# Sums of activations made over the second chunk and in the third chunk's first unit; the first down weights decoded two slots later

## The chip, the cores and the metric

The kernel runs on one core of a Trainium2 chip. The metric is the device time of one execution in microseconds (us). TensorE multiplies matrices (PE in the profile; PEld is its weight load), VectorE is DVE, ScalarE is ACT, GpSimd is POOL, and SP only issues transfers.

## The reference, cut to what matters

```
def phi(x):                                   # head_dim 64 -> 2 x 128 features
    proj = einsum('bhsd,df->bhsf', x, w_phi)
    proj = proj - max(abs(proj), axis=-1)
    return concatenate([exp(proj), exp(-proj)], axis=-1)
q_p, k_p = phi(q), phi(k)                     # batch 4, heads 8, seq 576
kv, z = einsum('bhsf,bhsd->bhfd', k_p, v), sum(k_p, axis=2)
attn = einsum('bhsf,bhfd->bhsd', q_p, kv) / (einsum('bhsf,bhf->bhs', q_p, z) + 1e-6)

x = attn as (2304 tokens, 512)
x = (sigmoid(x @ w_gate) * (x @ w_val)) @ w_out      # layer 1, d_ff 1536
h = x @ w_in2
out = maximum(0.01 * h, h) @ w_out2                  # layer 2, d_ff 2048
```

## The kernel before, in words

Every product of the two layers is made of three matmuls (`mm3`, L51 to L54): an operand is split into a high part that TensorE takes exactly and a low part that is the rest (`split`: a cast on ScalarE, L48, and a subtraction on VectorE, L49). The weights come from memory as 64-bit numbers and are decoded by `decode` (L97 to L114), per half of 128x512 six VectorE instructions (L102, L105, L107, L109, L111, L114) and two of ScalarE (L103, L112). `fetch` (L122) issues the load of such a half, `raw`.

Tokens stand as four blocks of 512 columns (b = 0 to 3, in two pairs) and a block B of 256 columns that holds the four rests. The hidden width is cut into chunks of 256: six chunks in layer 1, eight in layer 2. A chunk has the weights (layer, chunk, i) with i = 0 (gate), 1 (val), 2 (down).

The program has these parts, with the times of the profile before.

*Attention, 0 to about 290 us.* Sixteen pairs of heads run through slots; the order of the pieces in a slot is written by hand in `ORDERS` and `SLOTS` (L513 on). A piece `d` is one step of `first_weights`, which decodes chunk 0's three weights in slots 1 to 3; from slot KD = 4 on, pieces `M` run chunk 0's units of layer 1. `norm3` writes the attention's result to DRAM as `xd` as well.

*Chunk 0's rest and chunk 1, to about 395 us.* Plain units, one per block: `up_plain` (products into the banks `ps_u`, tanh on ScalarE L704, L706 on VectorE, `hidden`), then `down1_piece` per block and quarter (products into one of three banks `ps_p`). A down piece is copied by ScalarE into a staging half (L678) and added to DRAM by an accumulating transfer of POOL (L679, `accd`). There are six staging halves, used in turn.

*Chunks 2 to 5, to about 640 us.* For a pair of blocks `quad` makes the four products of 2x2 quarters out of seven instead of eight. It needs sums of weights (L176, L181) and sums of activations. The latter are made once for each pair: `load_x`-like transfers of SP bring `xd` into four tiles `acc` (L763, 512 KB each), `sum_steps` makes four subtractions on VectorE (L739), and `sum_parts` splits each result (ScalarE L749, VectorE L750); `store_sums` writes them to DRAM as `td`. Only one pair's sums are in SBUF at a time: `swap` loads the other pair's (L791, `w<-td`, on POOL) while a unit's products use up the old ones. Seven results are combined by additions of VectorE (L831). In chunk 1 all sums of layer 1 are made, pair 0's first, then pair 1's:

```
side.append(first_sums(0, False))
for b in range(NB):
    reserve[0] = (4, 8, 8, 5, 2)[b]
    if b == 2:
        for g in side:
            for _ in g:
                pass
        side[:] = [first_sums(1, True)]
    h = up_plain(1, 1, b, 5)
```

`side` holds generators whose steps `ahead` takes in between the units' pieces, beside one step of `stream`, which decodes the next weights as long as more than `reserve` of the 41 weight slots are free. A loop over `side` runs the rest of it at once.

*Step to layer 2, about 640 to 700 us.* In chunk 5 the sums of the down products stay in tiles `acc` (L682, added by VectorE), are split for block B and others (ScalarE L685, VectorE L686), and become the activations of layer 2, again with sums (L739, L749, L750): pair 0's four subtractions in the last unit, pair 1's four in front of layer 2.

*Layer 2, to the end.* Units of pair 0, block B and pair 1 per chunk, `quad` with one weight, results added by L901.

A tile framework's scheduler sets the static order on every engine; each engine then runs its instructions in that order.

## Time and profile before

| what | value |
| --- | --- |
| device time, three runs | 1053.50, 1058.68, 1058.72 us; median 1058.68 |
| the profiled execution | 1057.37 us |
| its span | 1055.6 us |
| mean granted TensorE clock | 0.997 |
| VectorE busy | 779.7 us |
| ScalarE busy | 519.4 us |

The span goes from the first to the last instruction that the profiler saw; the rest of the profiled execution's time lies around it. PEclk is the share of TensorE's full clock that was granted. In the table of stretches an engine's busy time stands beside the length of the stretch, so that the difference is its idle time there.

### The profile page before, as it was taken

The numbers are of one execution on the slowest core, as the hardware profiler recorded it, in microseconds if no ns is written. First come the engines' busy times: TensorE is split into PE (matmuls) and PEld (weight loads), VectorE is DVE, ScalarE is ACT, GpSimd is POOL, SyncE is SP. The second block draws the span as 40 slices with busy tenths as digits, with TensorE's granted clock in tenths as the row PEclk, the third lists the DMA queues.
The fourth block names the chain that finished last, engine by engine and source line by source line (L and its number), as shares of the span: only waits on it lengthen the run. The fifth ranks groups of instructions, "written<-read, shape, count | busy, mean of one in ns | idle before, by whom it ended". The sixth has DMA issues, their size and how long they took to land.

```text
span 1055.6 us, 15004 instructions
## 1 busy us (share of the span) xinstructions
PE 1024.2 (97%) x5410; PEld 870.9 (82%) x5410; DVE 779.7 (74%) x1373; ACT 519.4 (49%) x1066; POOL 170.2 (16%) x217
## 2 busy tenths in 40 slices
PE   8999999999999989999999999899999999999998
PEld 7788989889788778888888878688888888888886
DVE  4964878766489748396684959998797887979555
ACT  4766676767456535454454434477343333433221
POOL 0112121212201123324144120001010010101000
PEclk9999999999999999999999999999999999999999
DMA  6543344332287978759499494536161542515143
GB/s 146 157 98 90 88 101 108 82 104 75 74 296 226 343 141 246 114 145 262 73 239 195 82 317 182 182 139 228 52 237 71 171 149 91 178 62 179 42 165 133
DMA packets 119481, 160.06 MB, mean 152 GB/s; under 512 B 68720, under 2 KB 71408, under 8 KB 119408
## 3 DMA queue, kind: packets, MB, share of 16 engines
q1 hardware_dynamic: 95216, 94.09, 28.5%
q0 software_dynamic: 24192, 65.02, 24.6%
q8 instruction: 43, 0.70, 0.3%
q14 instruction: 30, 0.25, 0.1%
HBM read 109.64 MB, written 49.36 MB: 151 GB/s over the span
## 4 chain that ended last, share of the span: by engine, by line
PE 81%; DVE 8%; DMA 5%; ACT 3%; issue 2%; SPq 1%; POOL 1%; POOLq 0%; DVEq 0%; ACTq 0%
PE ps_u L53 11%; PE ps_u L52 11%; PE ps_u L54 11%; PE ps_p L52 11%; PE ps_p L54 11%; PE ps_p L53 11%; PE kv L395 4%; PE ps_n L445 2%; DMA raw<-in_moe_w_gate_dram 1%; DMA acc<-xd 1%; PE ps_t L328 1%; DVE w L750 1%; DVE ql L430 1%; DVE acc L739 1%; DMA w<-td 1%
## 5 line engine op out<-in xcount | busy, mean ns | idle before, releaser
L831 DVE TENSOR_TENSOR q<-ps_u,q 128x512 f32<-128x512 f32 x160 | 109.6, 686 | 65.6 <-PE ps_u L54 59.4
L53 PE MATMUL ps_u<-xl,w 128*128 128x512 f32 (+1 forms) x432 | 151.6, 351 | 0.3 <-DVE xl L686 0.3
L52 PE MATMUL ps_u<-xh,w 128*128 128x512 f32 (+1 forms) x432 | 151.4, 351 | 0.1
L54 PE MATMUL ps_u<-xh,w 128*128 128x512 f32 (+1 forms) x432 | 150.9, 350 | 0.0
L901 DVE TENSOR_TENSOR acc<-acc,ps_p 128x512 f32<-128x512 f32 x126 | 86.1, 684 | 39.6 <-PE ps_p L54 39.0
L52 PE MATMUL ps_p<-w,gh 128*128 128x512 f32 x288 | 112.2, 390 | 0.0
L53 PE MATMUL ps_p<-w,gh 128*128 128x512 f32 x288 | 112.0, 389 | 0.0
L54 PE MATMUL ps_p<-w,gl 128*128 128x512 f32 x288 | 111.7, 389 | 0.0
L791 POOL DMA_DIRECT2D w<-td x88 | 48.7, 560 | 380.6 <-PE ps_u L54 365.2
L679 POOL DMA_DIRECT2D accd<-w x80 | 70.8, 892 | 229.2 <-ACT w L678 148.3
L52 PE MATMUL ps_u<-w 128*128 128x512 f32 x256 | 100.2, 391 | 1.6 <-DVE q L831 1.6
L53 PE MATMUL ps_u<-w 128*128 128x512 f32 x256 | 99.9, 390 | 0.7 <-DMA w<-td 0.7
L54 PE MATMUL ps_u<-w 128*128 128x512 f32 x256 | 99.7, 389 | 0.0
L52 PEld LDWEIGHTS ps_u<-xh,w 128*128 128x128 f32 x432 | 81.9, 190 | 11.9 <-DVE q L831 0.5
L53 PEld LDWEIGHTS ps_u<-xl,w 128*128 128x128 f32 x432 | 82.0, 190 | 11.4 <-DVE xl L686 0.5
L54 PEld LDWEIGHTS ps_u<-xh,w 128*128 128x128 f32 x432 | 81.9, 190 | 10.9
L52 PE MATMUL ps_p<-gh,w 128*128 128x512 f32 (+1 forms) x216 | 79.3, 373 | 10.3 <-ACT gh L48 4.8
L467 POOL TENSOR_TENSOR rb<-u,rb 64x576 f32<-64x576 f32 x32 | 49.2, 1537 | 233.8 <-DMA rb<-rd 136.3
L717 ACT ACTIVATE q<-q 128x512 f32<-128x512 f32 x48 | 30.2, 632 | 111.9 <-DVE q L831 111.6
L53 PE MATMUL ps_p<-gl,w 128*128 128x512 f32 (+1 forms) x216 | 80.1, 372 | 0.4 <-DVE gl L49 0.4
L54 PE MATMUL ps_p<-gh,w 128*128 128x512 f32 (+1 forms) x216 | 79.7, 370 | 0.0
L49 DVE TENSOR_TENSOR gl<-q,gh 128x512 fp32r<-128x512 f32 (+1 forms) x102 | 61.8, 613 | 20.6 <-ACT gh L48 20.2
(151 smaller groups left out, 2306.0 us busy)
## 6 DMA issues: line engine op xcount, KB each, us to landing
w<-td POOLq DMA_DIRECT2D x88, 512.0 KB, 6.5
td<-w SPq DMA_DIRECT2D x32, 512.0 KB, 5.2
accd<-w POOLq DMA_DIRECT2D x64, 256.0 KB, 6.1
raw<-in_moe_w_out_dram SPq DMA_DIRECT2D x28, 512.0 KB, 4.8
raw<-in_moe_w_in_dram SPq DMA_DIRECT2D x16, 512.0 KB, 4.1
raw<-in_moe_w_gate_dram SPq DMA_DIRECT2D x12, 512.0 KB, 5.9
raw<-in_moe_w_val_dram SPq DMA_DIRECT2D x12, 512.0 KB, 5.1
rb<-rd SPq DMA_DIRECT2D x32, 144.0 KB, 3.2
```

Of the source, the lines that this page charges most:

```text
L49: nc.vector.tensor_tensor(out=lo, in0=src, in1=hi.bitcast(F32), op=ALU.subtract)
L52: nc.tensor.matmul(ps, lh, rh, start=first, stop=False, **kw)
L53: nc.tensor.matmul(ps, lh, rl, start=False, stop=False, **kw)
L54: nc.tensor.matmul(ps, ll, rh, start=False, stop=last, **kw)
L395: nc.tensor.matmul(ps[:, h], p.kf[j // 2][:, j % 2, h, s, :], vf[:, j, 64 * h:64 * h + 65], start=(h, j) == (0, 0), stop=False)
L445: nc.tensor.matmul(ps2, w[0], x[0], start=s == 0, stop=s == 1)
L467: nc.gpsimd.tensor_tensor(out=p.rb[sl], in0=p.u[h][sl], in1=p.rb[sl], op=ALU.mult)
L679: nc.gpsimd.dma_start(out=accd[b][:, e], in_=st, accum_op=ALU.add)
L717: nc.scalar.activation(out=th, in_=t, func=ACTF.Lrelu)
L791: nc.gpsimd.dma_start(out=ts[n][k][0].bitcast(F32), in_=td[l, pair, n][:, k])
L831: nc.vector.tensor_tensor(out=o, in0=x, in1=y, op=ALU.add)
L901: nc.vector.tensor_tensor(out=a, in0=a, in1=po, op=ALU.add)
```

## The change

The sums of pair 0 for layer 1 are no longer made in chunk 1; only pair 1's are, over the whole of that chunk, and with less of `reserve`. Pair 0's are made in the first unit of chunk 2 by a new generator `make_sums`, of which `used` tells which old sums have been read; their loads are issued by `load_x(0)` behind chunk 1. So `swap` always loads, and the eight loads of the first swap go away. The sums of layer 2 use the same generator: pair 0's in the last unit of chunk 5, pair 1's in the first unit of layer 2 instead of in front of it. In the attention, gate and val weights are decoded in slots 1 to 3 with fewer pieces `d`, and the down weights in slots 4 and 5 from one raw buffer; the tiles `tp` go from three to two buffers. There are four staging halves instead of six, one more `q` tile, and the tanh results of the pair units stand in `q` tiles. `room` lets down pieces stand between the seven products in other numbers.

```
     ORDERS = [
         "tq tk pk0 pk1 tr pq0 pkr ld pq1 pqr qr qf0 kv0 kv1 qf1",
-        "nn0 d tk tq d nn1 tr pk0 d d d pk1 nm3 nn2 d nn3 d pqr pq0 nm1 d pq1 d pkr d kv0 nm2 ld qr d d kv1 d qf0 qf1 d d",
-        "d tk nn0 d pk0 nn1 pk1 d tr nn2 d nn3 tq d pkr nm1 pqr ld d d pq0 d pq1 d kv0 d d qr d nm3 d nm2 qf0 qf1 kv1 d d",
+        "nn0 tk tq nn1 tr pk0 d pk1 nm3 nn2 d nn3 pqr pq0 nm1 d pq1 pkr d kv0 nm2 ld qr d kv1 qf0 qf1",
+        "tk nn0 pk0 nn1 pk1 d tr nn2 nn3 tq d pkr nm1 pqr ld pq0 d pq1 kv0 d qr nm3 d nm2 qf0 qf1 kv1",
...
-    dec = first_weights()
+    dec = first_weights((0, 1), 2)
...
             step(dec, 100)
...
-            pools["tp"] = mid.enter_context(tc.tile_pool(name="tp0", bufs=3))
+            pools["tp"] = mid.enter_context(tc.tile_pool(name="tp0", bufs=2))
+            pools["dec"] = mid.enter_context(tc.tile_pool(name="dec1", bufs=1))
+            dec = first_weights((2,), 1)
...
-                if 1 <= i < KD:
+                if 1 <= i <= KD + 1:
                     step(dec)
...
-        return halves[staged[0] % 6]
+        return halves[staged[0] % 4]
...
+    def make_sums(l, pair, used):
+
+        yield from sum_steps(l, pair)
+        late = None
+        for n in (2, 1, 3, 4):
+            while used is not None and n not in used:
+                yield True
+            ts[n] = [take(F32R) for _ in range(2)] if used is None else [retake(t) for t in ts[n]]
+            sum_parts(l, pair, n, ts[n])
+            yield True
+            yield True
+            if late:
+                store_sums(*late)
+            late = l, pair, n, ts[n]
+        for _ in range(2):
+            yield True
+        store_sums(*late)
+
+    def first_sums(pair):
+        load_x(pair)
         for _ in range(14):
             yield True
-        yield from sum_steps(1, pair)
...
+        yield from make_sums(1, pair, None)
...
-        for i, t in quad(1, c, 0, pair, (1, 1, 1, 1, 1, 0), lambda n: None):
-            th[i] = halves[6 + i]
+        for i, t in quad(1, c, 0, pair, (2, 1, 1, 1, 1, 0), lambda n: None):
+            th[i] = tile2() if i == 0 else t
...
-        for i, t in quad(1, c, 1, pair, (1, 1, 1, 0, 0, 0), then):
+        for i, t in quad(1, c, 1, pair, (1, 1, 0, 0, 0, 0), then):
...
-    side.append(first_sums(0, False))
+    side.append(first_sums(1))
     for b in range(NB):
-        reserve[0] = (4, 8, 8, 5, 2)[b]
-        if b == 2:
-            for g in side:
-                for _ in g:
-                    pass
-            side[:] = [first_sums(1, True)]
+        reserve[0] = (4, 4, 0, 0, 0)[b]
...
+    load_x(0)
...
+                if c == 2 and n == 0:
+                    used = set()
+                    side.append(make_sums(1, 0, used))
+                    h = up_pair1(c, u, done, used.add)
+                    finish()
...
-                    side.append(sum_steps(2, 0))
+                    side.append(make_sums(2, 0, used))
...
-    for _ in sum_steps(2, 1):
-        pass
...
+            elif c == n == 0:
+                used = set()
+                side.append(make_sums(2, 1, used))
+                h = up_pair2(c, u, used.add)
+                gap(100)
             else:
+                finish()
```

How instructions stand now, at three places. In these rows `w<-m`, `m<-raw` and `e<-raw` are the decoding of weights; the line numbers of the changed file differ (L347 and L349 are L351 and L353 there, L739 is L738, L750 is L749, L831 is L832, L682 and L686 are L681 and L685).

VectorE in the attention, third pair (slot 2), where the features' maxima (`m<-ps_p`) and differences (`t<-ps_p`) are made; before:

```order
L102 TENSOR_SCALAR e<-raw 128x512
L105 TENSOR_SCALAR m<-raw 128x512
L347 TENSOR_REDUCE m<-ps_p 128x4
L114 TENSOR_TENSOR w<-m,w 128x512
L107 SCALAR_TENSOR_TENSOR m<-raw,m 128x512
L109 SCALAR_TENSOR_TENSOR e<-raw,e 128x512
L349 TENSOR_TENSOR t<-ps_p,m 128x512
L111 SCALAR_TENSOR_TENSOR m<-m,e 128x512
L347 TENSOR_REDUCE m<-ps_p 128x4
L102 TENSOR_SCALAR e<-raw 128x512
L349 TENSOR_TENSOR t<-ps_p,m 128x512
```

and in the changed kernel:

```order
L114 TENSOR_TENSOR w<-m,w 128x512
L351 TENSOR_REDUCE m<-ps_p 128x4 x2
L353 TENSOR_TENSOR t<-ps_p,m 128x512 x2
L109 SCALAR_TENSOR_TENSOR e<-raw,e 128x512
L105 TENSOR_SCALAR m<-raw 128x512
L111 SCALAR_TENSOR_TENSOR m<-m,e 128x512
L351 TENSOR_REDUCE m<-ps_p 128x2 x2
L353 TENSOR_TENSOR tr<-ps_p,m 128x256
L353 TENSOR_TENSOR tqr<-ps_p,m 128x256
L49 TENSOR_TENSOR xl_79<-rb,xh_78 128x512
```

Between the first two maxima stood four decoding instructions; now two maxima and their differences follow one another, and three decoding instructions stand behind them.

VectorE at the beginning of chunk 2's first unit, around the first additions of `quad` (`q<-ps_u,q`); before:

```order
L49 TENSOR_TENSOR gl<-q,gh 128x256
L114 TENSOR_TENSOR w<-m,w 128x512 x2
L706 SCALAR_TENSOR_TENSOR q<-q,ps_u 128x256
L105 TENSOR_SCALAR m<-raw 128x512 x2
L49 TENSOR_TENSOR gl<-q,gh 128x256
L107 SCALAR_TENSOR_TENSOR m<-raw,m 128x512 x2
L831 TENSOR_TENSOR q<-ps_u,q 128x512
L111 SCALAR_TENSOR_TENSOR m<-m,e 128x512 x2
L102 TENSOR_SCALAR e<-raw 128x512
L114 TENSOR_TENSOR w<-m,w 128x512 x2
```

and in the changed kernel:

```order
L705 SCALAR_TENSOR_TENSOR q<-q,ps_u 128x256
L49 TENSOR_TENSOR gl<-q,gh 128x256
L832 TENSOR_TENSOR q<-ps_u,q 128x512
L738 TENSOR_TENSOR acc<-acc 128x1024 x4
L832 TENSOR_TENSOR q<-ps_u,q 128x512
L114 TENSOR_TENSOR w<-m,w 128x512
L832 TENSOR_TENSOR q<-ps_u,q 128x512
L114 TENSOR_TENSOR w<-m,w 128x512
L832 TENSOR_TENSOR q<-ps_u,q 128x512
L180 TENSOR_TENSOR m<-m 128x2x128 x2
L832 TENSOR_TENSOR q<-ps_u,q 128x512
```

The four subtractions of pair 0's sums now stand between the first and the second addition.

VectorE at the step to layer 2; before:

```order
L686 TENSOR_TENSOR xl_93<-acc,xh_92 128x512 x2
L739 TENSOR_TENSOR acc<-acc 128x1024
L831 TENSOR_TENSOR q<-ps_u,q 128x512
L739 TENSOR_TENSOR acc<-acc 128x1024
L105 TENSOR_SCALAR m<-raw 128x512
L739 TENSOR_TENSOR acc<-acc 128x1024
L107 SCALAR_TENSOR_TENSOR m<-raw,m 128x512
L739 TENSOR_TENSOR acc<-acc 128x1024
L750 TENSOR_TENSOR w<-acc,w 128x1024
L682 TENSOR_TENSOR acc<-acc,ps_p 128x256 x2
L750 TENSOR_TENSOR w<-acc,w 128x1024
L686 TENSOR_TENSOR xl_95<-acc,xh_94 128x256 x2
```

and in the changed kernel:

```order
L685 TENSOR_TENSOR xl_93<-acc,xh_92 128x512 x2
L832 TENSOR_TENSOR q<-ps_u,q 128x512
L738 TENSOR_TENSOR acc<-acc 128x1024
L105 TENSOR_SCALAR m<-raw 128x512
L738 TENSOR_TENSOR acc<-acc 128x1024
L107 SCALAR_TENSOR_TENSOR m<-raw,m 128x512
L738 TENSOR_TENSOR acc<-acc 128x1024
L681 TENSOR_TENSOR acc<-acc,ps_p 128x256
L738 TENSOR_TENSOR acc<-acc 128x1024
L685 TENSOR_TENSOR xl_95<-acc,xh_94 128x256
L681 TENSOR_TENSOR acc<-acc,ps_p 128x256
L749 TENSOR_TENSOR w<-acc,w 128x1024
L685 TENSOR_TENSOR xl_95<-acc,xh_94 128x256
```

The addition `q<-ps_u,q` now stands ahead of the subtractions, and one `acc<-acc,ps_p` and one `xl<-acc,xh` stand between the third, the fourth and the first split.

## Rows read from the trace of the kernel before

**Rows 1.** The page, busy time of each engine: us (share of the span) and instructions.

```profile
PE 1024.2 (97%) x5410; PEld 870.9 (82%) x5410; DVE 779.7 (74%) x1373; ACT 519.4 (49%) x1066; POOL 170.2 (16%) x217
```

**Rows 2.** The page, shares of the chain that ended last, by engine.

```profile
PE 81%; DVE 8%; DMA 5%; ACT 3%; issue 2%; SPq 1%; POOL 1%; POOLq 0%; DVEq 0%; ACTq 0%
```

**Rows 3.** Busy time by stretch: PE, PEld, DVE, ACT, POOL (instructions), PEclk, DMA share, GB/s.

```profile
340.00:361.00 21.00, 21.00 (x94) 17.41 (x93) 15.05 (x20) 9.35 (x14) 3.48 (x4) 1.00 1.05 332
361.00:385.00 24.00, 18.92 (x86) 14.64 (x86) 16.41 (x30) 10.60 (x19) 3.63 (x4) 0.96 0.85 243
385.00:400.00 15.00, 15.00 (x84) 13.19 (x83) 8.46 (x17) 6.65 (x13) 5.32 (x6) 0.95 0.83 149
600.00:640.00 40.00, 38.09 (x167) 30.90 (x166) 25.78 (x43) 15.69 (x28) 9.64 (x14) 1.00 0.89 254
...
676.00:692.00 16.00, 11.23 (x56) 9.25 (x55) 15.84 (x25) 8.12 (x12) 0.00 (x0) 0.89 0.59 220
...
760.00:1000.00 240.00, 240.00 (x1116) 201.13 (x1116) 197.10 (x347) 93.27 (x160) 22.66 (x42) 1.00 0.37 127
```

**Rows 4.** Waits of TensorE, 340 to 400: total us, times, longest.

```profile
PE ps_p L52 <- ACT gh L48: 3.4, 2, 3.0
```

**Rows 5.** Timeline of TensorE: start us, us, instruction, [idle before <- releaser].

```profile
378.66 0.40 PE L53 MATMUL ps_p<-gl,w 128*128 128x512 f32 x1
378.89 0.39 PE L54 MATMUL ps_p<-gh,w 128*128 128x512 f32 x1
382.31 0.51 PE L52 MATMUL ps_p<-gh,w 128*128 128x512 f32 x1 [3.03 <-ACT gh L48]
```

**Rows 6.** The chain of waits, 340 to 400: start us, us, what.

```profile
344.44 9.95 DMA acc<-xd
...
372.26 6.74 DMA raw<-in_moe_w_gate_dram
```

**Rows 7.** Waits of TensorE, 600 to 700.

```profile
PE ps_p L52 <- DVE acc L682: 4.1, 1, 4.1
PE ps_u L52 <- DVE q L831: 1.6, 2, 1.2
```

**Rows 8.** Busy time by stretch in the attention (columns as in rows 3).

```profile
24.00:37.00 13.00, 12.41 (x93) 11.38 (x92) 11.40 (x21) 9.24 (x22) 0.00 (x0) 1.00 0.63 159
37.00:58.00 21.00, 17.81 (x99) 13.36 (x98) 19.03 (x37) 14.24 (x37) 2.95 (x2) 1.00 0.50 131
58.00:72.00 14.00, 13.99 (x102) 12.44 (x100) 7.67 (x14) 8.86 (x25) 2.83 (x2) 1.00 0.37 96
```

**Rows 9.** Timeline of VectorE at the step to layer 2.

```profile
679.03 0.42 DVE L105 TENSOR_SCALAR m<-raw 128x512 int32<-128x512 int32 x1
679.37 1.21 DVE L739 TENSOR_TENSOR acc<-acc 128x1024 f32<-128x1024 f32 x1
680.50 0.68 DVE L107 SCALAR_TENSOR_TENSOR m<-raw,m 128x512 f32<-128x512 uint32 x1
681.11 1.21 DVE L739 TENSOR_TENSOR acc<-acc 128x1024 f32<-128x1024 f32 x1
```

**Rows 10.** Tile acc, 295 to 365: the loads acc<-xd.

```profile
L763 SPq DMA_DIRECT2D acc<-xd x8: 432/878/1493, 296.7 to 344.4; - x8
...
DMA to landing us min/median/max: 6.9/8.2/10.0
```

**Rows 11.** The page, DMA issues: xcount, KB each, median us to landing.

```profile
w<-td POOLq DMA_DIRECT2D x88, 512.0 KB, 6.5
```

**Rows 12.** Waits of VectorE, 600 to 640.

```profile
DVE e L102 <- DMA raw<-in_moe_w_out_dram: 6.0, 1, 6.0
```

**Rows 13.** Timeline of ScalarE's L678, 488 to 498.

```profile
488.69 0.59 ACT L678 COPY w<-ps_p 128x512 f32<-128x512 f32 x1 [0.51 <-ACT gh L48]
490.05 0.59 ACT L678 COPY w<-ps_p 128x512 f32<-128x512 f32 x1 [0.77 <-PE ps_p L54]
...
491.41 0.59 ACT L678 COPY w<-ps_p 128x512 f32<-128x512 f32 x1 [0.15 <-ACT e L103]
...
496.56 1.07 ACT L678 COPY w<-ps_p 128x512 f32<-128x512 f32 x2
```

**Rows 14.** Tile accd, 290 to 640: the accumulating transfers' landing.

```profile
L679 POOL DMA_DIRECT2D accd<-w x80: 854/873/1261, 332.1 to 623.4; - x80
...
DMA to landing us min/median/max: 1.7/5.9/9.3
```

More of the change, by code (lines that the diff above doesn't have):

```diff
@@ L126, in fetch, with first_weights @@
         return raw
-    def first_weights():
-        for i in range(3):
+    def first_weights(which, bufs):
+        for i in which:
             _, w, expo = weight(1, 0, i)
             r = {k: take(F32R) for k in ("hi", "lo")}
-            raws = [fetch((1, 0, i), j) for j in range(2)]
+            raws = deque(fetch((1, 0, i), j, bufs) for j in range(bufs))
             yield
-            for j, raw in enumerate(raws):
+            for j in range(2):
+                if not raws:
+                    raws.append(fetch((1, 0, i), j, bufs))
+                    yield
+                raw = raws.popleft()
                 cs = slice(512 * j, 512 * j + 512)
@@ L591, in tile2 @@
         return pools["q"].tile([128, 512], F32, tag="q", name="q")[:, :w]
-    fixed, halves = [], []
-    def fix(n):
-        for _ in range(n):
-            s = take(F32)
-            fixed.append(s)
-            halves.extend(s[0][:, 512 * i:512 * i + 512] for i in range(2))
-    fix(3)
+    fixed = [take(F32) for _ in range(2)]
+    halves = [s[0][:, 512 * i:512 * i + 512] for s in fixed for i in range(2)]
     staged = [0]
@@ L756, in store_sums, with load_x, finish @@
             nc.sync.dma_start(out=td[l, pair, n][:, k], in_=s[k][0].bitcast(F32))
-    def first_sums(pair, stay):
+    def load_x(pair):
         for i in range(2):
             for j in range(2):
-                s = sums[0, 2 * pair + i, j] = take(F32, "acc")
-                nc.sync.dma_start(out=s[0].rearrange("p (k t) -> p k t", k=2), in_=xd[2 * pair + i][:, 2 * j:2 * j + 2])
+                t = sums[0, 2 * pair + i, j] = take(F32, "acc")
+                nc.sync.dma_start(out=t[0].rearrange("p (k t) -> p k t", k=2), in_=xd[2 * pair + i][:, 2 * j:2 * j + 2])
+    def make_sums(l, pair, used):
[16 more added lines that the diff above has]
+        load_x(pair)
         for _ in range(14):
             yield True
-        yield from sum_steps(1, pair)
-        held = deque()
-        def put():
-            n, s = held.popleft()
-            store_sums(1, pair, n, s)
-            if not stay:
-                give(*s)
-        for n in (2, 1, 3, 4):
-            s = [take(F32R) for _ in range(2)]
-            sum_parts(1, pair, n, s)
-            if stay:
-                ts[n] = s
-            held.append((n, s))
-            yield True
-            yield True
-            if len(held) == 2:
-                put()
-        for _ in range(4):
-            yield True
-        put()
+        yield from make_sums(1, pair, None)
+    def finish():
+        for g in side:
+            for _ in g:
+                pass
+        side.clear()
     def load_sums(l, pair, n):
@@ L967, in between @@
                     drop_sums(1, c, 0)
-                    give(*fixed[:3])
-                    side.append(sum_steps(2, 0))
-                def then(k):
-                    for g in side:
-                        for _ in g:
-                            pass
-                    side.clear()
-                    swap(2, 0, k)
+                    give(*fixed)
+                    side.append(make_sums(2, 0, used))
                 load_acc(0)
@@ L979, in linear_attention_moe @@
                 hold[0] = 2, 1
-                h = up_pair1(c, 1, between, then)
+                h = up_pair1(c, 1, between, used.add)
+                finish()
                 drop_sums(1, c, 1)
```

21 lines of the change are left out of this document (7 added, 14 removed), and 4 rows, old and new, of the table ORDERS.

## Prediction

> **What bounds the kernel now.** I read the page's totals first, then the chain of waits, then a table of busy time by stretch, and last the waits, timelines and transfers of the stretches that lose time. TensorE is busy 97% of the span and VectorE 74% [rows 1]; the chain that ended last is 81% TensorE, 8% VectorE and 5% DMA [rows 2]. So time is won only where TensorE stands still, or runs at half clock (1.2 instead of 2.4 GHz) after it stood still. In the long stretch from 760 to 1000 us it is busy 240.00 of 240.00 us [rows 3]: nothing there. Three places that the change touches do lose time.
>
> In chunk 1, TensorE is busy 18.92 of 24 us between 361 and 385, with a mean granted clock of 0.96 there and 0.95 in the 15 us behind [rows 3]. The longest single wait is 3.0 us [rows 4], between 378.89 and 382.31 [rows 5]. The chain through it is: a sum's load `acc<-xd` in flight for 9.95 us from 344.44, the subtractions behind it, then a raw weight load of 6.74 us that was issued only at 372.26 [rows 6]. Just before, from 340 to 361, the DMA share is 1.05, the only stretch of the table where the transfers fill their engines [rows 3].
>
> At the step from layer 1 to layer 2, 676 to 692, TensorE is busy 11.23 of 16 us at a clock of 0.89, while VectorE is busy 15.84 [rows 3]: VectorE is the bound. The wait is 4.1 us on L682 [rows 7], which stands behind four L739 subtractions and an L750.
>
> In the attention's third pair, 37 to 58 us, VectorE is busy 19.03 of 21 us and TensorE 17.81; the pieces before and behind take 13 and 14 us with a like amount of matmuls (93, 99 and 102) and 11.40 and 7.67 us of VectorE [rows 8]. That slot is VectorE's too, by some 6 us.
>
> **The change part by part.** VectorE's price for one instruction is taken from start to start, as its records overlap: L739 1.14 us (679.37 to 680.50), a 512-wide L107 0.60, an L105 mask 0.34 [rows 9]. In the changed file L739, L750, L831 and L682 are L738, L749, L832 and L681.
>
> *Attention.* By the order, decoding instructions on VectorE in the first five slots go from 0, 7, 11, 18, 0 and then none to 0, 7, 7, 13, 6 and then 3, counted by pair. Six decode one half: four of 0.60 and two of 0.34, so 0.51 each. The third pair's slot loses 5 x 0.51 = 2.6 us of work, the slot before it 2.0 us. The nine that move come to slots where VectorE works 7.67 of 14 us [rows 8], so they are hidden on average; if that cover failed they would cost 9 x 0.51 = 4.6. I take a gain of 3.0: the 2.6 where VectorE is the bound, and a little for a smaller backlog at its start. Ends: a gain of 4.6 (all nine) and a loss of 1.5 (a pause like the third pair's appears in a later one).
>
> *Chunk 1's second set of sums.* It leaves this stretch whole: four loads, four L739, four L750. Without them the raw loads aren't late, and VectorE isn't blocked. What can come back is the idle 24.00 - 18.92 = 5.1 us, and the half clock: 0.04 x 24 + 0.05 x 15 = 1.7 us [rows 3]. The printed wait is short of the true hole: 382.31 - 378.89 less the usual 0.23 is 3.19 for a printed 3.03 [rows 5], so five waits hide another 0.8. Together 7.6, and I take all of it, since load, sums and their store all go. Ends: nothing, and 8.2 (with the smaller waits around).
>
> *Chunk 2's first unit.* The sums now stand here. The loads of xd0 and xd1 wait for slots of chunk 1's weights. By the order the last is issued once block B's products of chunk 1 are done, and L832, for which the product into px waits, stands behind the four subtractions. From there TensorE has 30 matmuls of 0.23 [rows 5] and 25 of half that width, so half that time: 9.8 us of cover. The chain is a load's issue 0.5, its landing, three L738 of 1.14 and an L832 of 0.60, so 4.5 plus the landing. Such loads landed in 6.9 to 10.0 us, median 8.2 [rows 10]; those were taken while the transfers were full, and other transfers of that size took less, 6.5 for `w<-td` [rows 11]. With 6.5 the stall is 1.2 us, with 8.2 it is 2.9. I take 2.0. Ends: nothing, and 10.0 + 4.5 - 9.8 = 4.7 plus 1.7 of half clock, 6.4.
>
> The Trainium skill ("SBUF — State Buffer", the section on the DMA setup-cost knee) gives a transfer as about 2 us plus its bytes at 436 GB/s, an estimate of 3.2 us for 512 KB. By it there would be no stall here and the sum would be 2.0 lower; the rows of this kernel are at twice that and more [rows 10, 11], and they decide.
>
> *The 1.2 us at 613.* VectorE waits 6.0 us there for a raw load [rows 12], and TensorE 1.2 for the L831 behind it [rows 7]. The stream of weights is no longer held up by the reserve of chunk 1, and its fetches come earlier. I take a gain of 1.2. Ends: 0 and 1.6.
>
> *The step to layer 2.* The same sums are made, but the order puts the first L832 ahead of the subtractions, L681 one subtraction earlier, and hands layer 2's second set to its first unit instead of in front of it. It loses 16 - 11.23 = 4.8 us and 0.11 x 16 = 1.8 at half clock, with 0.5 unprinted 7.1 in all. Counted in the order at the prices above, VectorE's work from 640 us to layer 2's second unit falls only from 57 to 55 us, against 51 of TensorE's matmuls; it stays the bound, and the product into px still waits for an L832 behind an L749, an L114 and an L681. I put the instructions of both engines at those prices one behind the other in the new order: waits of 0.8, 1.5 and 3.0 stay, 5.3 us, and perhaps a short spell of half clock. So I take a gain of 1.5. Ends: a gain of 5.5 and a loss of 1.0.
>
> *With no price.* The eight loads `w<-td` of td10 that go away were waited for nowhere in chunk 2. Four staging halves instead of six: below. Two attention staging tiles instead of three and seven q tiles: nothing in the rows waits for them.
>
> The sum: -3.0 - 7.6 + 2.0 - 1.2 - 1.5 = -11.3. The profiled execution took 1057.37 us, so 1046.1. It lies 0.12% below the median of 1058.68, between the runs shown.
>
> **The rivals.** *The hole moves.* The loads for chunk 2's first unit land as slowly as the slowest one did, 10.0 us, and the stall is 6.4 instead of 2.0: 1050.5. For it speaks that three loads start at almost the same moment, next to weight loads; against it that the DMA has more room than at 340 to 361. *The VectorE-bound places give nothing back*, as the work only moves by a few us: the attention and the step to layer 2 gain 0 instead of 4.5, 1050.6. *The change doesn't do what it says in chunk 1*: the raw gate load comes late by itself, and the wait of 3.2 and the half clock of 1.7 stay: 1051.0. The chain speaks for it, since its last DMA piece is that load [rows 6]; but that load waited for its buffer behind the sums. *Slower:* the four staging halves. L678, in order on ScalarE, must wait until the accumulating transfer from four copies before has landed. Four copies apart is 8.3 us where they stand closest (488.69 to the second of the two from 496.56 on, three in between) [rows 13], and with 0.6 for the copy itself and 0.9 for the issue a landing of up to 6.8 is free. They take 5.9 in the median and 9.3 at most [rows 14]. TensorE's two other banks hold off another 2.7. So it decides from landings of some 9.5 us on, that is if they get slower than any in this trace; if half of the 48 pair-wide copies of chunks 2 to 4 then waited 0.7 us, 16.8 us would come on top: 1063.
>
> **How the numbers follow.** The forecast of 1046 has a chance of 0.67, the moved hole 0.12, the VectorE-bound places 0.10, the gate load 0.06, slower staging 0.05. All but the last are faster by over 0.5% (5.3 us, about what a measurement of this kernel can tell), if they come alone; two of the middle ones together give 1055, no change. I put 0.82 on faster, 0.13 on the same, 0.05 on slower. The range goes from 1038 (1.6 more from the attention, the 2.0 of chunk 2's stall, and 4.0 more at the step to layer 2, 7.6 in all) to 1055 (two of the middle rivals).
>
> **What would show it.** Right: the stretch from 361 to 400 with TensorE fully busy at clock 1.00; the third pair's slot near 17 us; L832 waits of 1 to 3 us in chunk 2's first unit; and at the step to layer 2 still some 5 us of waits. Wrong: a wait for the raw gate load in chunk 1, waits for `acc<-xd` of over 4 us with a clock below 1 behind them, or ScalarE's L677 waiting for POOL's transfers.

## The result, and where the time went

The changed kernel takes 1075.64 us in the median of four runs (1069.62 to 1077.27) against 1058.70 for the kernel before beside it (four runs, 1053.50 to 1062.04). The ratio is 1.0146, with a 95% interval of 1.0116 to 1.0176: slower by 1.5%, where 1046.1 was predicted and the range ended at 1055. The profiled execution took 1069.62 us, its span is 1067.8 at a mean granted clock of 0.992; the three others took 1075 to 1077 at 0.984, so part of the loss is half clock that this profile shows only in part.

Both traces hold 5410 matmuls, so the start of the n-th matmul in one trace can be set against the n-th in the other. The table is worked out from the two traces in that way; a difference above zero means that the changed kernel is later. In the attention some pieces stand in another order than before, so the first three differences are good to some 0.7 us. From the end of the attention on, the points are taken where both kernels have the same work behind them.

| matmul | place | start before, us | difference, us |
| --- | --- | --- | --- |
| 293 | attention, fourth pair begins | 58.3 | -4.8 |
| 499 | sixth pair begins | 87.8 | -3.1 |
| 712 | eighth pair begins | 119.9 | +1.8 |
| 1883 | attention ended, chunk 1's first unit | 296.7 | +4.2 |
| 2183 | chunk 1, block 3 | 359.2 | +5.3 |
| 2315 | chunk 2's first unit begins | 392.2 | -2.8 |
| 2718 | chunk 3's first unit, ahead of the hole | 473.5 | +3.3 |
| 2783 | behind it | 485.7 | +9.2 |
| 3143 | chunk 4's first unit, behind its hole | 559.8 | +13.2 |
| 3483 | chunk 5 | 634.4 | +12.4 |
| 3723 | step to layer 2 | 687.2 | +8.0 |
| 3783 | layer 2's first unit | 700.3 | +12.2 |
| 5383 | close to the end | 1045.3 | +12.2 |

Chunk 1 gave nearly what was hoped for, 7.0 us from matmul 1883 to 2315. The attention lost 4.2, chunk 2's first unit 6.1, the first units of chunks 3 and 4 together 9.9; 0.8 came back in chunks 4 and 5, and the step to layer 2 came out even. The stretches of the changed kernel, columns as in [rows 3]:

```profile
37.00:58.00 21.00, 20.20 (x122) 16.76 (x122) 19.54 (x36) 14.77 (x38) 3.15 (x2) 1.00 0.49 122
...
84.00:103.00 19.00, 16.85 (x103) 14.66 (x103) 8.80 (x16) 9.76 (x25) 2.82 (x2) 0.91 0.28 71
361.00:385.00 24.00, 24.00 (x119) 20.32 (x118) 13.52 (x25) 10.03 (x18) 4.42 (x5) 1.00 0.76 154
398.00:412.00 14.00, 9.81 (x38) 7.70 (x37) 10.70 (x16) 5.41 (x9) 1.76 (x2) 0.88 0.26 34
480.00:492.00 12.00, 7.98 (x28) 6.12 (x27) 7.67 (x14) 2.90 (x5) 4.26 (x8) 0.86 1.01 326
555.00:567.00 12.00, 8.23 (x46) 6.89 (x45) 8.21 (x16) 3.13 (x6) 3.74 (x7) 1.00 1.03 335
...
686.00:702.00 16.00, 12.31 (x55) 9.67 (x54) 15.38 (x24) 7.58 (x11) 0.00 (x0) 0.83 0.59 230
```

From 361 to 385 TensorE is now busy for 24.00 of 24 us at full clock, where [rows 3] had 18.92 and 0.96. But 398 to 412, 480 to 492 and 555 to 567 each have about 4 us of idle time. TensorE's waits from 395 to 565 are three, all of one kind; none of them is in the trace of before:

```profile
PE ps_u L52 <- DVE q L832: 12.0, 3, 4.2
```

In the chain that ended last TensorE's share fell from 81% [rows 2] to 59%, and POOL's rose from 1% to 8%; much of the rest is "issue". From 400 to 640 us that chain now runs along POOL's transfers, so it does not show the holes; the waits above do:

```profile
PE 59%; issue 18%; POOL 8%; DVE 5%; DMA 4%; ACT 3%; SPq 2%; POOLq 0%; ACTq 0%
```

**The two late holes.** VectorE, from 479 on (start, duration, instruction, idle time before it and what ended it), in the changed kernel's timeline:

```profile
479.98 0.69 DVE L109 SCALAR_TENSOR_TENSOR e<-raw,e 128x512 int32<-128x512 int32 x1 [0.24 <-ACT e L103]
484.71 0.43 DVE L102 TENSOR_SCALAR e<-raw 128x512 int32<-128x512 int32 x1 [4.03 <-DMA raw<-in_moe_w_out_dram]
485.05 1.29 DVE L114 TENSOR_TENSOR w<-m,w 128x512 fp32r<-128x512 f32 x2
486.25 0.69 DVE L109 SCALAR_TENSOR_TENSOR e<-raw,e 128x512 int32<-128x512 int32 x1
486.86 0.69 DVE L832 TENSOR_TENSOR q<-ps_u,q 128x512 f32<-128x512 f32 x1
```

SP's transfers in the timeline of the same stretch:

```profile
477.03 0.34 SPq L122 DMA_DIRECT2D raw<-in_moe_w_out_dram  x1
478.83 0.38 SPq L122 DMA_DIRECT2D raw<-in_moe_w_gate_dram  x1
```

The second half of the down weights goes out at 477.03, and VectorE's L102 stands before it from 480.7 to 484.71. L832, for which the next product needs its bank, is four instructions further on in the same queue. The same two instructions in the kernel before, first SP's load in the timeline:

```profile
487.80 0.34 SPq L122 DMA_DIRECT2D raw<-in_moe_w_out_dram  x1
```

and VectorE's wait for it:

```profile
493.97 0.43 DVE L102 TENSOR_SCALAR e<-raw 128x512 int32<-128x512 int32 x1 [1.99 <-DMA raw<-in_moe_w_out_dram]
```

There the load goes out at 487.80, in block B, and VectorE waits 1.99 us with no L831 behind it that anyone waits for: TensorE has no wait between 395 and 565 in that trace. Between the issue of the fetch and VectorE's turn at its L102, 21 matmuls began in the kernel before and 16 begin now. The distance had always been short; it was the place that changed.

**Chunk 2's first unit** has the hole that the prediction expected, but larger. SP issues the last three of the four loads at the end of chunk 1, and VectorE's subtractions wait for them. SP in the timeline of the changed kernel:

```profile
387.95 1.76 SPq L762 DMA_DIRECT2D acc<-xd  x3
```

The tile `acc`, 376 to 400, has the four loads' landing:

```profile
DMA to landing us min/median/max: 7.1/8.5/9.5
```

VectorE:

```profile
397.57 1.23 DVE L738 TENSOR_TENSOR acc<-acc 128x1024 f32<-128x1024 f32 x1 [4.55 <-DMA acc<-xd]
399.03 3.74 DVE L738 TENSOR_TENSOR acc<-acc 128x1024 f32<-128x1024 f32 x3 [0.23 <-DMA acc<-xd]
402.69 0.68 DVE L832 TENSOR_TENSOR q<-ps_u,q 128x512 f32<-128x512 f32 x1
```

TensorE:

```profile
398.86 0.39 PE L54 MATMUL ps_u<-xh,w 128*128 128x512 f32 x1
403.43 0.80 PE L52 MATMUL ps_u<-w 128*128 128x512 f32 x1 [4.19 <-DVE q L832]
404.02 0.63 PE L53 MATMUL ps_u<-w 128*128 128x512 f32 x1
404.45 0.63 PE L54 MATMUL ps_u<-w 128*128 128x512 f32 x1
```

The first subtraction starts at 397.57, 9.6 us after the first of the three was issued. The other three start from 399.03 on, when the last load, issued at 389.39, has landed after 9.5 us, and L832 follows at 402.69. TensorE's last matmul ahead of the hole starts at 398.86, the next at 403.43; then its 512-wide matmuls stand 0.43 us apart instead of 0.23, at half clock.

**The attention** gains in the third pair, as forecast: 37 to 58 us has 122 matmuls instead of 99 [rows 8]. It gives that back later. TensorE waits for the normalised block (`xh`, ScalarE) before the first product of a unit of chunk 0, and at 84 to 103 the clock is 0.91:

```profile
PE pg L52 <- ACT xh L48: 3.6, 2, 2.1
```

Between the same pairs the kernel before had this wait once:

```profile
PE pg L52 <- ACT xh L48: 1.1, 1, 1.1
```

### The profile page after: what moved, and what is told of

It reads as the page before. It is cut to its first block, busy times and chain, and to the rows that moved or that the text cites. A ratio compares the mean times of both kernels' runs of the same rounds, so it can differ in the third digit from the quotient of the medians.

```text
span 1067.8 us, 14960 instructions
## 1 busy us (share of the span) xinstructions
PE 1026.7 (96%) x5410; PEld 872.2 (82%) x5410; DVE 778.0 (73%) x1373; ACT 517.7 (48%) x1066; POOL 165.5 (15%) x209
## 4 chain that ended last, share of the span: by engine, by line
PE 59%; issue 18%; POOL 8%; DVE 5%; DMA 4%; ACT 3%; SPq 2%; POOLq 0%; ACTq 0%
PE ps_p L52 9%; PE ps_p L54 8%; PE ps_p L53 8%; PE ps_u L52 8%; PE ps_u L53 8%; PE ps_u L54 7%; POOL accd L678 5%; PE kv L399 4%; POOL rb L471 1%; DMA raw<-in_moe_w_gate_dram 1%; DMA rb<-rd 1%; POOL w L796 1%; PE ps_n L449 1%; DVE ql L434 1%; DMA w<-td 1%
## 5 line engine op out<-in xcount | busy, mean ns | idle before, releaser
L832 DVE TENSOR_TENSOR q<-ps_u,q 128x512 f32<-128x512 f32 x160 | 110.0, 687 | 59.9 <-PE ps_u L54 51.0
L52 PE MATMUL ps_u<-w 128*128 128x512 f32 x256 | 101.7, 397 | 12.4 <-DVE q L832 12.0
L678 POOL DMA_DIRECT2D accd<-w x80 | 71.3, 946 | 248.0 <-ACT w L677 146.0
L796 POOL DMA_DIRECT2D w<-td x80 | 44.1, 556 | 374.5 <-PE ps_u L54 267.8
L53 PE MATMUL ps_u<-w 128*128 128x512 f32 x256 | 101.1, 395 | 0.7 <-DMA w<-td 0.7
L48 ACT CAST gh<-q 128x512 fp32r<-128x512 f32 (+1 forms) x134 | 75.1, 575 | 53.4 <-DVE q L879 35.9
L54 PE MATMUL ps_u<-w 128*128 128x512 f32 x256 | 100.9, 394 | 0.0
L49 DVE TENSOR_TENSOR gl<-q,gh 128x512 fp32r<-128x512 f32 (+1 forms) x134 | 82.9, 632 | 20.0 <-ACT gh L48 19.9
L52 PE MATMUL ps_p<-gh,w 128*128 128x512 f32 (+1 forms) x216 | 77.0, 368 | 2.9 <-ACT gh L48 1.3
```

The lines of the kernel that those rows point to most:

```text
L48: nc.scalar.copy(hi, src)
L49: nc.vector.tensor_tensor(out=lo, in0=src, in1=hi.bitcast(F32), op=ALU.subtract)
L52: nc.tensor.matmul(ps, lh, rh, start=first, stop=False, **kw)
L53: nc.tensor.matmul(ps, lh, rl, start=False, stop=False, **kw)
L54: nc.tensor.matmul(ps, ll, rh, start=False, stop=last, **kw)
L678: nc.gpsimd.dma_start(out=accd[b][:, e], in_=st, accum_op=ALU.add)
```

## The experiments

Times are medians with ratios to the kernel before, run on the same chip; differences at a matmul are worked out from traces as in the table. The median of the changed kernel, 1075.64, is the measure for the single edits. The runs stand on several chips, and the median of the kernel before lies between 1058.47 and 1061.24 us beside them, so small differences are safer as ratios.

**The late fetches.** Theory: the change frees three weight slots (one that held two of the staging halves, and two that held the tanh results, now in `q` tiles), the decoding of the next weights then runs ahead, and the fetch lands in the middle of the loads of stored sums. First run: the three slots are taken out of the rotation.

```
+            if c == 2 and n == 1:
+                parked = [free.popleft() for _ in range(3)]
...
                     give(*fixed)
+                    free.extend(parked)
```

> The changed kernel with three weight slots taken out of the rotation from chunk 2's block B to chunk 5's last unit, as many as the staging halves held before. Theory (more free slots let the decoding of weights run ahead, and the second half of the down weights is then fetched 15 matmuls before VectorE wants it, in the middle of the loads of stored sums): the two holes of 4.2 us at 483 and 3.9 us at 558, with half clock behind them, go; 9.8 us less, a span of about 1058. Rival (the transfers are too many at that place wherever the fetch stands): the holes stay or move, span within 3 us of 1067.8.

Measured: 1066.77 us, ratio 1.0078 (1.0054 to 1.0102), 8.9 us less than the changed kernel. From matmul 2718 to 3143 the difference to before stays as it was, where the changed kernel lost 9.9. Two smaller waits for L832 came up elsewhere, 1.4 us at 452 and 1.9 at 622, and the profiled execution is only 3.2 us shorter, as the attention and chunk 2's first unit lost more in this trace (6.6 and 7.4). The two holes are gone with the freed slots, then, and the place of the fetch is what moved: the late half of the down weights goes out at the 2784th matmul here, in block B and close to the 2792nd of the kernel before, while the changed kernel has it at the 2718th.

Second run: the free slots stay, but the stream has four raw buffers instead of three, paid for with one weight slot, so that each fetch goes out a half earlier.

```
-        raws = deque(fetch(keys[n // 2], n % 2, 3) for n in range(3))
+        raws = deque(fetch(keys[n // 2], n % 2, 4) for n in range(4))
...
-                ahead = 2 * n + i + 3
+                ahead = 2 * n + i + 4
...
-    NSLOT = 41
+    NSLOT = 40
```

> The changed kernel with four raw buffers for the stream of weights instead of three, paid for with one of the 41 weight slots. Each fetch then goes out one half earlier: the second half of the down weights 61 matmuls ahead of its use instead of 15, while the use itself, the loads of stored sums and the free slots that let the stream run ahead stay. Theory (VectorE stands before a raw load that was fetched too late): both holes, at 483 and 558, go although the load still meets the loads of stored sums; 10 us or more less, time about 1065. Rival (it is the collision of transfers and not the lead): the load still lands 7 to 8 us after its issue and something else waits, the holes stay over 2 us.

Measured: 1061.47 us, ratio 1.0018 (0.9997 to 1.0038), 14.2 us less than the changed kernel in the median and 10.9 between the two profiled executions. In this trace the transfers of that stretch are no faster than in the changed kernel, where they took 4.2 to 9.8 us; the view of the tile `raw` from 455 to 490:

```profile
L122 SPq DMA_DIRECT2D raw<-in_moe_w_out_dram x2: 340/340/341, 462.3 to 465.4; - x2
...
DMA to landing us min/median/max: 4.5/8.3/10.5
```

TensorE's waits in it, 395 to 640:

```profile
PE ps_u L52 <- DVE q L832: 3.6, 2, 3.5
PE ps_u L53 <- DMA w<-td: 0.7, 1, 0.7
```

The raw loads of this stretch take 4.5 to 10.5 us, 8.3 in the median, and TensorE waits for none of them: both halves of the down weights went out by 465.4. The only large wait left is chunk 2's. That speaks against the rival: at this place the collision remains, and the lead was missing. A run with 40 slots and three buffers was not made, so what the slot given up does by itself isn't known.

**The attention.** The changed kernel with the attention of before:

```
-    dec = first_weights((0, 1), 2)
+    dec = first_weights()
...
-            pools["tp"] = mid.enter_context(tc.tile_pool(name="tp0", bufs=2))
-            pools["dec"] = mid.enter_context(tc.tile_pool(name="dec1", bufs=1))
-            dec = first_weights((2,), 1)
+            pools["tp"] = mid.enter_context(tc.tile_pool(name="tp0", bufs=3))
...
-                if 1 <= i <= KD + 1:
+                if 1 <= i < KD:
```

with the old `first_weights` and the old rows of `ORDERS`.

> The changed kernel with the attention of before: all three first weights decoded in slots 1 to 3, the same orders, three staging tiles. Theory (the decoding of the down weights in slots 4 and 5 and the faster slots ahead of it delay the normalisation's chain, which costs 8.9 us after a gain of 4.8): the attention ends 4.2 us earlier, span about 1063.6. Rival (the changed attention gains, and the loss comes from the units of chunk 0 that run beside it): no gain, span 1067 to 1070.

Measured: 1067.96 us, ratio 1.0089 (1.0069 to 1.0110), 7.7 us less than the changed kernel. At matmul 1883 the difference to before is -0.5 instead of +4.2. The wait before `pg` is 0.2 us. So the change in the attention costs, 4.7 us by these two traces. The other runs bear it out: those with the changed attention as it is stand 4.2 to 6.6 us behind at that matmul, those with the attention of before between 1.2 ahead and 1.3 behind. The whole profiled execution is only 1.5 us shorter than the changed kernel's, because the hole in chunk 4's first unit cost 7.2 us in this trace instead of 4.0, with a wait of 5.3 instead of 3.8 and half clock behind it; that the medians differ by more than 4.7 may be the half clock of the changed kernel's other runs.

What delays the block? In the changed kernel the reciprocals of the normalisation are ready at 80.7 and leave SP only at 83.60, behind the loads of v; the broadcast loads follow at 86.33, 5.6 us after the reciprocals. In the kernel before, the same step takes 2.3 us, from 85.5 to 87.82. In the changed kernel:

```profile
81.63 0.56 SPq L314 DMA_DIRECT2D vf<-in_v_dram  x1
...
83.60 0.57 SPq L465 DMA_DIRECT2D rd<-r  x1
...
86.33 1.22 SPq L468 DMA_DIRECT2D rb<-rd  x2
```

So the transfers of the normalisation were put on POOL's queue:

```
-        nc.sync.dma_start(out=rd.rearrange("h (p e) -> (h p) e", e=9), in_=r)
+        nc.gpsimd.dma_start(out=rd.rearrange("h (p e) -> (h p) e", e=9), in_=r)
...
-            nc.sync.dma_start(out=p.rb[64 * h:64 * h + 64], in_=rd[h:h + 1, :].to_broadcast([64, S]))
+            nc.gpsimd.dma_start(out=p.rb[64 * h:64 * h + 64], in_=rd[h:h + 1, :].to_broadcast([64, S]))
```

> The changed kernel in which the attention's normalisation issues its small transfers (the reciprocals to DRAM and their two broadcast loads) from POOL's queue and not from SP's, where the reciprocals stand behind the next pair's v loads (in the changed kernel they are ready at 80.7 and leave at 83.6). Theory (that queue delays the chain to the first units of chunk 0): the holes of 1.7 and 2.3 us before the products into pg shrink by 2 us or more in all and the half clock behind the second one goes, the attention ends 3 to 4 us earlier. Rival (VectorE's later decoding delays the reciprocals themselves): under 1 us.

Measured: 1073.67 us, ratio 1.0135 (1.0096 to 1.0174), not to be told from the changed kernel. The trace is clearer than the time; TensorE's waits of over 1 us between 53 and 125:

```profile
PE kv L399 <- ACT ka L360: 2.2, 1, 2.2
```

Both waits before `pg` are gone, and a new one of 2.2 us stands at 60, where ScalarE's queue now holds the copy of `xh` ahead of `ka`. At matmul 712 the kernel is 0.9 us behind before instead of 1.8. SP's queue is one link of the delay, then; the chain through the normalisation is longer than the order allows for, and which engine is made to wait depends on where the order puts the copy. Which of the attention's edits brings this about was not separated further.

**Chunk 2's first unit.** Three of the four loads ahead of chunk 1's block B, and the fourth subtraction put back by eight steps:

```
+        if b == B:
+            load_x(0, ((0, 0), (1, 0), (1, 1)))
...
+            if l == 1 and pair == 0 and o is b21:
+                for _ in range(8):
+                    yield True
...
-    load_x(0)
+    load_x(0, ((0, 1),))
```

> The changed kernel with three of the four loads of pair 0's activations issued ahead of chunk 1's block B instead of behind it, the fourth as soon as one slot of chunk 1's weights is free. Theory (the subtractions wait for loads that start too late): the hole of 4.4 us at 399 and its half clock shrink to at most 1.5 us, span 1062 to 1063. Rival (VectorE then stands before the earlier loads in block B): a hole of 2 to 4 us comes up between 375 and 395, span 1066 or more.

Measured: 1074.90 us, ratio 1.0157 (1.0137 to 1.0177), no gain. Chunk 2's hole shrank as the theory has it, but a new one came at 354. TensorE's waits, 340 to 420:

```profile
PE ps_p L52 <- ACT w L677: 3.8, 1, 3.8
PE ps_u L52 <- DVE q L835: 2.3, 3, 1.4
```

VectorE's only wait from 340 to 362:

```profile
DVE e L102 <- DMA raw<-in_moe_w_out_dram: 5.8, 1, 5.8
```

It is once more a raw load of down weights behind which VectorE stands, with a short lead: issued at 345.31, wanted at 350.2. In the changed kernel the same load had the same 4.9 us of lead, landed in 7.6 us, and cost VectorE 2.8 us and TensorE 0.9. Here the first of the early loads, issued at 343.51, is in flight beside it. The transfers issued from 344 to 358 in this run, with KB and us to landing (the load of 343.51 is counted in):

```profile
acc<-xd SPq DMA_DIRECT2D x1, 512.0 KB, 11.1
raw<-in_moe_w_out_dram SPq DMA_DIRECT2D x1, 512.0 KB, 10.5
```

So at this place a fetch with a short lead and a collision came together.

**The staging halves**, the rival on the slower side: six again, for one more slot.

```
-    fixed = [take(F32) for _ in range(2)]
+    fixed = [take(F32) for _ in range(3)]
...
-        return halves[staged[0] % 4]
+        return halves[staged[0] % 6]
```

> The changed kernel with six staging halves again, one more weight slot for them. Theory (four halves cost nothing beyond the 1.1 us hole at 354): that hole goes, the rest stays, time 1073 to 1076. Rival of the prediction (ScalarE's copies wait for accumulating transfers, and L876 and L48 behind them reach TensorE late): waits of L677 for accd vanish and with them 3 us or more, time 1072 or less.

Measured: 1072.76 us, ratio 1.0121 (1.0086 to 1.0156), just below what the theory gives and above the rival's 1072; the interval overlaps that of the changed kernel. In the changed kernel ScalarE's L677 does wait for accumulating transfers, and with six halves not at all. Its waits for them from 340 to 640 in the changed kernel:

```profile
ACT w L677 <- DMA accd<-w: 15.0, 11, 2.9
```

All 11 stand behind 395, and none of these 15 us shows as a wait of TensorE: its waits from 395 to 640 are L832's three, above. The rival's wait was real and hidden.

**The edits together.** First those of the parked slots, the attention and the three early loads.

> The three edits of the other runs together. If the three causes are independent: 9.8, 4.2 and about 5 us less than the changed kernel, span about 1049, so 6 us below before, ratio to before about 0.994. If they share a cause (the transfers), the gain is under 12 us and the ratio 1.000 or more.

Measured: 1061.28 us, ratio 1.0025 (1.0009 to 1.0042). That is 14.4 us less than the changed kernel and less than was expected of the parts; smaller waits for L832 (L829 in that file) of 1.2 to 1.8 us were left at 392, 444, 583 and 615.

Then those of the four raw buffers and of the attention.

> Four raw buffers and the attention of before, the rest of the change kept. If both causes are as the single runs say, the span is about 1053: 9.8 us for the late fetches, 4.5 for the attention, and the hole of chunk 2's first unit with its half clock (6 us) still there; ratio to before about 0.997. If the fetches collide anyway: 1060 or more.

Measured: 1057.34 us, ratio 0.9985 (0.9961 to 1.0009). TensorE's wait in chunk 2's first unit was still there, 5.3 us. So two of its loads went ahead, on top:

```
+        if b == B:
+            load_x(0, ((0, 0), (1, 0)))
...
-    load_x(0)
+    load_x(0, ((1, 1), (0, 1)))
```

> The run before (four raw buffers, the attention of before) with two of pair 0's four loads issued ahead of chunk 1's block B, those that the first subtraction needs, and the other two as soon as slots are free. Theory (the four loads start within 13 matmuls of each other and too late for the subtractions): the hole of 5.4 us at 395 and its half clock shrink to 1 to 3 us, 3 to 5 us in all, span about 1053, ratio 0.995. Rival (VectorE waits as long for the last two as for all four): no change, 1057.

Measured: 1055.74 us, ratio 0.9973 (0.9952 to 0.9994). TensorE's waits from 360 to 420 are down to 2.1 us in two:

```profile
PE ps_u L52 <- DVE q L829: 2.1, 2, 1.1
```

This is the change without its part in the attention, with the late fetches and the late loads mended, and it is faster than before by a quarter of a per cent.

**The step to layer 2.** Its waits moved, and the step did not get shorter. Before, TensorE waited 4.1 us for L682 [rows 7]. In the changed kernel it waits for `xh` and `xl` of block B, at a clock of 0.83; the longest wait there:

```profile
PE ps_u L52 <- ACT xh L684: 2.4, 1, 2.4
```

To take work from VectorE, the eight subtractions went to POOL, in the kernel with four raw buffers and the attention of before (1057.34 us).

```
-            nc.vector.tensor_tensor(out=o, in0=x, in1=y, op=ALU.subtract)
+            (nc.gpsimd if l == 2 else nc.vector).tensor_tensor(out=o, in0=x, in1=y, op=ALU.subtract)
```

> The run before (four raw buffers, the attention of before) with the eight subtractions of layer 2's sums on POOL, which does nothing between 640 and 700, and not on VectorE. Theory (VectorE's work bounds the step to layer 2, and where it stands in it only moves the holes): 4 to 5 us of VectorE's work go from the stretch ahead of layer 2 and the holes there, 4.1 us and 3.4 of half clock, shrink to under 3 in all; span about 1053. Rival (the chain of splits and adds bounds it, and POOL's slower subtractions lengthen it: 1.5 us for 64x576 speaks for 2.7 for 128x1024): the same or slower, 1057 to 1062.

Measured: 1064.67 us, ratio 1.0048 (1.0028 to 1.0068), 7.3 us more than without. That is slower than even the rival gave (1057 to 1062), and not for its reason alone: VectorE got no emptier. From 640 to 700 it is busy 58.15 us with the subtractions on POOL and 57.16 with them on itself. Two rows of POOL's timeline:

```profile
643.24 2.71 POOL L732 TENSOR_TENSOR acc<-acc 128x1024 f32<-128x1024 f32 x1 [2.48 <-issue]
646.98 5.49 POOL L732 TENSOR_TENSOR acc<-acc 128x1024 f32<-128x1024 f32 x2 [1.03 <-DVE xl L679]
```

and five of VectorE's beside them:

```profile
643.62 2.61 DVE L105 TENSOR_SCALAR m<-raw 128x512 int32<-128x512 int32 x1
646.15 0.68 DVE L679 TENSOR_TENSOR xl<-acc,xh 128x512 fp32r<-128x512 f32 x1
...
647.36 0.68 DVE L826 TENSOR_TENSOR q<-ps_u,q 128x512 f32<-128x512 f32 x1
647.96 2.26 DVE L111 SCALAR_TENSOR_TENSOR m<-m,e 128x512 f32<-128x512 f32 x1
650.14 2.60 DVE L105 TENSOR_SCALAR m<-raw 128x512 int32<-128x512 int32 x1
```

An L105 that takes 0.42 us [rows 9] takes 2.61 and 2.60 here, an L111 2.26 instead of 0.68. Each ends 0.3 to 0.5 us behind the end of a subtraction of POOL (taking the two of the second row as equally long). L826, which reads a PSUM bank, took 0.68 in the middle of one.

**Two last runs.** The normalisation on POOL's queue (its diff above), on top of the best run so far:

> Four raw buffers, the attention of before, two early loads, and the normalisation's small transfers on POOL's queue. Theory (in the attention of before the same transfers stand behind the pairs' loads on SP too, and cost the 1.3 us before pg and parts of the waits between 140 and 200): 1 to 3 us less than without, span 1047 to 1049, ratio 0.993 to 0.996. Rival (as in the changed kernel, one product of an earlier slot then waits behind ScalarE's copy of the normalised block): no gain or up to 5 us lost, 1050 to 1056.

Measured: 1068.24 us, ratio 1.0068 (1.0031 to 1.0106). The first product into `pg` moved ahead in the order, from the 265th matmul to the 227th, and TensorE waited 4.1 us before it at 45, for `xh`. The rival was right in kind, but the loss against 0.9973 is about 10 us, twice the 5 that it allowed: by the 293rd matmul this trace is already 8.4 us behind before.

And the control: the kernel before with nothing of the change's sums, but four raw buffers, for which one weight slot and one slot of two staging halves were given up (the stream's lines as above, and these):

```
-    NSLOT = 41
+    NSLOT = 40
...
-    fix(3)
+    fix(2)
...
-        return halves[staged[0] % 6]
+        return halves[staged[0] % 4]
...
-            th[i] = halves[6 + i]
+            th[i] = halves[4 + i]
```

> The kernel before with four raw buffers, paid for with one weight slot and one of the slots that held staging halves (four halves instead of six). Nothing of the change's sums is in it. If the wait in chunk 1 was the late raw load's (its fetch now goes out one half earlier), the hole of 3.2 us at 379 with its half clock goes as well as the 1.4 us at 613, and this kernel is 5 to 7 us faster than before, as fast as or faster than the best run so far: ratio 0.994. If it was the sums' loads and the blocked VectorE, the hole at 379 stays over 2 us and the ratio lies between 0.998 and 1.001.

Measured: 1052.77 us in eight runs, ratio 0.9940 (0.9915 to 0.9965), the fastest of all; the profiled execution had a mean clock of 1.000, the other seven 0.993 to 0.997. Its stretches, columns as in [rows 3]:

```profile
340.00:361.00 21.00, 21.00 (x94) 17.40 (x93) 16.41 (x25) 10.38 (x15) 3.49 (x4) 1.00 1.05 319
361.00:385.00 24.00, 22.01 (x106) 17.82 (x105) 16.52 (x29) 11.83 (x20) 5.38 (x6) 1.00 0.96 275
385.00:400.00 15.00, 15.00 (x90) 13.33 (x89) 11.60 (x24) 8.73 (x17) 5.45 (x6) 1.00 0.83 161
600.00:640.00 40.00, 39.46 (x174) 32.36 (x173) 27.46 (x45) 15.98 (x27) 8.41 (x13) 1.00 0.71 221
676.00:692.00 16.00, 14.12 (x72) 11.54 (x73) 15.56 (x29) 11.06 (x21) 0.00 (x0) 1.00 0.77 258
```

VectorE's two longest waits from 340 to 400 in it:

```profile
DVE w L114 <- ACT w L112: 6.0, 1, 6.0
DVE acc L739 <- DMA acc<-xd: 4.4, 1, 4.4
```

VectorE still waits 4.4 us for the sums' load, and the DMA share from 340 to 361 is the same 1.05 as in [rows 3]; but VectorE's wait for the raw gate load, 3.2 us in the kernel before, is gone, TensorE is busy 22.01 of 24 us, and the clock stays at 1.00. From matmul 2183 to 2315 this kernel gains 5.3 us on before, the changed one 8.1. The best version with the change in it has 0.9973, and the two intervals overlap (0.9952 to 0.9994 and 0.9915 to 0.9965): with the lead in place, no run shows that moving the sums adds anything.

## Why the prediction was wrong, step by step

The sum was -11.3; the profiled execution is 12.25 us later than before. The parts measured from the table add up to it: +4.2 in the attention, -7.0 in chunk 1, +6.1 in chunk 2's first unit, +9.9 in the first units of chunks 3 and 4, -0.8 up to chunk 5 and -0.2 at the step to layer 2.

**Chunk 1, a gain of 7.6: right in size** (7.0 from matmul 1883 to 2315), and half right in cause. The prediction laid the hole to the sums, and gave the raw gate load a chance of 0.06 as a cause of its own. The control shows that 5.3 us go with an earlier fetch and the sums in place. Either edit breaks the chain of [rows 6].

**The step that failed** is the one on the stream of weights: "The stream of weights is no longer held up by the reserve of chunk 1, and its fetches come earlier. I take a gain of 1.2." The gain came (0.8). What the prediction left out is that a stream that runs earlier has its short-lead fetches at other places. They stood in block B, where nobody waits for VectorE; they came to stand between L832s and beside the loads of stored sums. That cost 9.9 us in the profiled execution, and with one more raw buffer 14.2 us of the median went. It is the largest part of the 23.5 us by which the sum missed; the attention's 7.2 and the 4.1 of chunk 2's first unit come next. The freed slots were in the diff, and that such fetches come late showed in the rows of before as VectorE's 6.0 us for a raw load [rows 12]; the prediction's own working followed only the loads of activations to their new place.

**The attention, a gain of 3.0 with ends of +1.5 and -4.6: wrong in sign,** a loss of 4.2. The gain in the third pair came (4.8 by the fourth pair). The step that failed is "so they are hidden on average". What the runs show in its place is two waits of 3.6 us in all before `pg`, for a block that comes late through the normalisation's chain of SP, POOL and ScalarE. That chain was not in the working at all. The two waits are not the whole loss, and which edit of the attention delays the chain stays open.

**Chunk 2's first unit, a loss of 2.0: right in mechanism, too small.** It lost 6.1, just inside the upper end of 6.4. The term that was mis-sized is the landing: 6.5 to 8.2 us were counted, and the last load took 9.5. The rest of the chain stood as written, three subtractions and an L832 behind that landing: the cover came out at 9.7 us for 9.8, the wait at 4.2, and the half clock, which the 2.0 left out, makes up the rest. The rival "the hole moves" had 0.12 and came true, close to its price of 4.4 more.

**The step to layer 2, a gain of 1.5:** 0.2. VectorE remained the busiest engine, 15.38 of 16 us, as was said; the walk by hand did not have the 2.4 us for ScalarE's `xh` of block B, at the end of the step.

**The staging halves, as a rival:** the wait is there and is hidden. The landings of the accumulating transfers stayed at 5.8 us in the median and 9.9 at most, so hardly one reached the 9.5 us from which the prediction saw a cost.

The Trainium skill ("SBUF — State Buffer", the section on the DMA setup-cost knee) would have put the landing of 512 KB at an estimate of 3.2 us; the loads of [rows 10] and the 8.3 us of the run with four raw buffers stand against it where several transfers are in flight. Going by the rows was right, and the upper rows were the ones to take: 7.1 to 9.5 us for the loads of chunk 2's first unit.

## What to carry to other kernels

When a change gives buffers back or takes them, look up for every prefetch how far ahead of its use it is now issued, in work of the engine that waits, and what that engine has behind it in its queue: a fetch 16 matmuls ahead of its use, with 7.6 us to land, is a hole waiting for a place to appear. One more buffer for the prefetch can be worth more than moving the work around it; here it gave 14.2 us to the changed kernel and 0.6% to the one before, with the slots that it cost paid. And hidden work is hidden only if the chain through every in-order queue still ends in time; busy shares don't show that.

## What the runs showed of the hardware

A VectorE instruction whose operands all lie in SBUF stood still while POOL subtracted two SBUF tiles: L105 took 2.61 us instead of 0.42, L111 2.26 instead of 0.68, each ending 0.3 to 0.5 us behind one of POOL's, while L826 with an operand in PSUM kept its 0.68. The Trainium skill says so ("SBUF — State Buffer", the section on who interferes with whom): a VectorE instruction with two SBUF inputs and a GpSimd instruction that reads SBUF exclude each other, so does a VectorE instruction in a two-port mode with GpSimd, and the later one waits. The trace agrees, with these numbers.

The price of a hole in half clock is not fixed. In the profile of the changed kernel the holes at 399 and 483 left clocks of 0.88 and 0.86 in their stretches, the one at 558 of nearly the same length (3.8 us of wait beside 4.2 and 4.0) left 1.00; the unprofiled runs of the same kernel were 5.5 to 7.7 us longer at a mean clock of 0.984 instead of 0.992. In the profile of the control, with no wait of TensorE over 2.5 us behind the attention, the clock was 1.000.
